# Queueing a block's gate-times-value product behind the next score's relu, loading the square-root table early, and turning the gains on TensorE

## The chip, the cores and the metric

The kernel runs on one core of one Trainium2 chip. The metric is the device time of one execution in microseconds (us). Most executions of one kernel lie here within a microsecond or two of each other; one first execution of the kernel before took 559.56 us. It is left out of every ratio, but the median of 443.69 us quoted below still counts it (the other three runs have 443.52). All runs recorded with a state are in the fast one. PE is the TensorE matmul engine, DVE is VectorE, ACT is ScalarE, SP issues most of the small transfers.

## The reference, cut to what matters

```python
# q, k, v: 8 batches, 12 heads, 448 positions, 64 wide
scores = q @ k.T / sqrt(64)
attn   = maximum(scores, 0) ** 2 / 448 @ v       # no softmax: relu, squared
x      = attn, heads side by side                # 3584 x 768
xn     = x / sqrt(mean(x * x) + 1e-6) * rms_g    # a norm over each row
g, val = xn @ w_gate, xn @ w_val                 # 768 -> 1536
out    = (silu(g) * val) @ w_out                 # 1536 -> 768
```

## The kernel before: the parts that matter

The kernel weaves two streams. While PE computes the gate and value blocks of batch b, pieces of batch b+1's attention are put between them. A block is one 128-wide slice of the 1536 hidden columns. It is 12 rounds of two matmuls, one for gate (psG) and one for value (psV), which run side by side on the two halves of the array's rows. In batches 1 to 7 it is issued in pieces of two rounds:

```python
def blocnpart(b, fb, r0, r1):
    if r0 == 0:
        gvs[b, fb] = [ps_m.tile([P, S], FP32, name=nm, tag="mm")[:] for nm in ("psG", "psV")]
    rounds(b, fb, gvs[b, fb], r0, r1)
    if r1 < 2 * KT:
        return
    psG, psV = gvs.pop((b, fb))
    s = spool.tile([P, S], BF16, name="sil", tag="sil")
    nc.scalar.activation(out=s[:], in_=psG, func=ACT.Silu)
    hT, o = hidden(b)
    nc.vector.tensor_tensor(out=hT[:, fb, o : o + S], in0=s[:], in1=psV, op=ALU.mult)
```

The pool `ps_m` has four buffers in PSUM, the memory that PE's results go to, so two blocks' worth: block n+2 takes the buffers of block n. A score has its own pool with two buffers; a relu empties it, on ACT, or on DVE for the second half of every odd head:

```python
    if on_dve:
        nc.vector.tensor_relu(out=r[:, cp], in_=src)
    else:
        nc.scalar.activation(out=r[:, cp], in_=src, func=ACT.Relu)
```

After a batch's attention, `leave` reads the last attention outputs on ACT, two pieces of an output projection follow on PE (their copies are on ACT), and then the norm: a square root on ACT, a reciprocal on DVE, six products of x, and DMAs that swap the halves of x into xD. The second six rounds of a block read xD.

## Time and profile before

| | before |
|---|---|
| median, first comparison | 443.69 us (4 runs, 443.1 to 559.56; 443.52 without the 559.56) |
| profiled execution | 443.02 us, span 441.2 us |
| first score on PE | 6.73 us |
| batches 1 to 7 on PE | 53.08, 49.11, 53.78, 49.12, 53.01, 49.12, 43.38 us |

A batch is measured on PE from the first instruction after one batch's output pieces to the first one after the next's. Odd batches carry four output tiles, even ones three, and batch 7 has no attention beside it. (The prediction's 53.85 us for batch 3 took the chain's entry at 242.40; PE's first score is at 242.33, so the length is 53.78.) The profile's lines are shown in the prediction.

### The profile page before, as it was taken

To read this page: it belongs to the slowest core of one execution; us is meant where nothing else is said; L and a number is where in the kernel's file an instruction comes from. 1 tells how busy PE (TensorE), PEld (TensorE's weight loads), DVE (VectorE), ACT (ScalarE), POOL (GpSimd) and SP (SyncE) were. 2 spreads that over 40 slices of the span, in tenths; PEclk is the share of its full clock that TensorE was granted. 3 is DMA by queue.
4 is the path that set the end of the run, shared out by engine and by line. 5 is a ranking of instruction groups with operands and counts; after the bars stand their busy time and mean duration, and the time that the engine had idled before them with its cause. 6 is when DMAs were issued, how large, how long until landed. Compare 5 with 4: busy or idle time off the path is not lost.

```text
span 441.2 us, 10928 instructions
## 1 busy us (share of the span) xinstructions
PE 431.9 (98%) x4718; PEld 248.6 (56%) x4718; DVE 288.8 (65%) x387; ACT 287.6 (65%) x445; POOL 53.7 (12%) x79
## 2 busy tenths in 40 slices
PE   7999999999999999999999999999999999999996
PEld 3345555655566555655566555655557555665664
DVE  4989975777863867766864768577775468742211
ACT  4899886676584775777765776767766677552220
POOL 8343300030001200021000300003000000000000
PEclk9999999999999999999999999999999999999999
DMA  9999999999117991189904997169903900041013
GB/s 135 196 207 198 197 211 186 199 177 182 33 37 157 208 153 33 37 182 169 149 15 96 188 207 95 36 108 224 164 18 78 206 20 1 1 116 57 1 37 109
DMA packets 87632, 53.21 MB, mean 121 GB/s; under 512 B 36768, under 2 KB 83232, under 8 KB 87584
## 3 DMA queue, kind: packets, MB, share of 16 engines
q0 software_dynamic: 44496, 27.50, 43.2%
q1 hardware_dynamic: 42464, 24.44, 28.1%
q8 instruction: 37, 0.61, 0.6%
q10 hardware_dynamic: 624, 0.57, 0.4%
q14 instruction: 11, 0.09, 0.1%
HBM read 47.19 MB, written 11.01 MB: 132 GB/s over the span
## 4 chain that ended last, share of the span: by engine, by line
PE 86%; ACT 7%; DVE 4%; issue 1%; DMA 1%; SPq 0%; ACTq 0%; DVEq 0%
PE psG L520 30%; PE psO L435 23%; PE psV L520 13%; PE psAV L273 9%; PE psS L228 6%; ACT r L217 2%; PE psW L663 2%; DVE r L240 1%; PE psS L187 1%; ACT r L197 1%; ACT sil L564 1%; DVE hT L566 1%; DMA xD<-xT 1%; DVE xT L500 1%; PE psT L143 1%
## 5 line engine op out<-in xcount | busy, mean ns | idle before, releaser
L520 PEld LDWEIGHTS <-wgv_sb 64*128 64x128 bf16 x2304 | 125.2, 94 | 95.6 <-issue 8.3
L520 PE MATMUL psV<-xD,wgv_sb 64*128 64x448 bf16 x558 | 128.4, 349 | 0.4 <-DMA xD<-xT 0.4
L520 PE MATMUL psG<-xD,wgv_sb 64*128 64x448 bf16 x558 | 128.5, 349 | 0.0
L520 PE MATMUL psG<-xT,wgv_sb 64*128 64x448 bf16 x558 | 128.4, 349 | 0.0
L520 PE MATMUL psV<-xT,wgv_sb 64*128 64x448 bf16 x558 | 128.0, 349 | 0.1
L242 ACT ACTIVATE r<-psS 112x896 bf16<-112x896 f32 x108 | 99.1, 918 | 20.5 <-PE psS L228 17.9
L435 PE MATMUL psO<-wo_sb,hT 128*64 128x512 bf16 (+2 forms) x1368 | 111.8, 323 | 0.0
L566 DVE TENSOR_TENSOR hT<-sil,psV 128x448 bf16<-128x448 bf16 x93 | 57.4, 618 | 62.6 <-ACT sil L564 62.6
L246 DVE TENSOR_TENSOR r<-r 112x1792 bf16<-112x1792 bf16 x72 | 78.0, 1088 | 29.2 <-ACT r L242 28.8
L435 PEld LDWEIGHTS <-hT 128*64 128x64 bf16 x1368 | 74.9, 110 | 35.6 <-issue 0.4
L564 ACT ACTIVATE sil<-psG 128x448 bf16<-128x448 f32 x93 | 50.5, 543 | 58.6 <-PE psV L520 35.5
L228 PE MATMUL psS<-qT,kT 64*128 64x448 bf16 (+1 forms) x288 | 56.1, 350 | 0.4
L587 ACT COPY ost<-psO 128x512 f32<-128x512 f32 (+1 forms) x54 | 25.1, 477 | 39.8 <-PE psO L435 39.8
L273 PE MATMUL psAV<-r,vb 112*64 112x448 bf16 x384 | 40.3, 355 | 0.0
L240 DVE TENSOR_SCALAR r<-psS 112x896 bf16<-112x896 f32 x36 | 39.0, 1084 | 1.9 <-PE psS L228 1.9
L175 POOL DMA_DIRECT2D qT<-qT x12 | 6.5, 541 | 263.5 <-PE psS L228 154.1
L273 PEld LDWEIGHTS <-vb 112*64 112x64 bf16 x384 | 20.1, 109 | 18.6 <-issue 6.5
L329 ACT ACTIVATE xT<-psAV,ga_sb 128x448 bf16<-128x448 f32 x47 | 27.8, 647 | 3.9 <-PE psAV L273 3.8
L228 PEld LDWEIGHTS <-kT 64*128 64x128 bf16 (+1 forms) x288 | 19.0, 97 | 16.0 <-issue 4.9
L500 DVE TENSOR_TENSOR xT<-xT,rstd 128x448 bf16<-128x448 bf16 x48 | 26.4, 619 | 2.3 <-ACT rstd L488 2.3
L471 DVE RECIPROCAL rhalf<-rhalf 128x224 f32<-128x224 f32 x8 | 12.4, 1553 | 21.3 <-ACT rhalf L465 21.3
L256 DVE TENSOR_TENSOR r<-r 112x1792 bf16<-112x1792 bf16 x23 | 24.3, 1083 | 0.7 <-ACT r L217 0.7
(68 smaller groups left out, 278.4 us busy)
## 6 DMA issues: line engine op xcount, KB each, us to landing
vb<-in_v_dram POOLq DMA_DIRECT2D x7, 672.0 KB, 18.4
xD<-xT SPq DMA_DIRECT2D x42, 112.0 KB, 2.3
qb<-in_q_dram POOLq DMA_DIRECT2D x6, 672.0 KB, 11.9
kb<-in_k_dram POOLq DMA_DIRECT2D x6, 672.0 KB, 14.5
qT<-qT POOLq DMA_DIRECT2D x24, 168.0 KB, 3.4
out_dram<-ost SPq DMA_DIRECT2D x7, 336.0 KB, 4.7
wgv_sb<-in_moe_w_gate_dram POOLq DMA_DIRECT2D x6, 384.0 KB, 16.9
wgv_sb<-in_moe_w_val_dram POOLq DMA_DIRECT2D x6, 384.0 KB, 16.9
```

Of the source, the lines that this page charges most:

```text
L228: nc.tensor.matmul(out=psS[: end - o, hf, :S], lhsT=flat[prt, o:end], rhs=qT[prt, 1 - hf : 3 - hf, h % HH], start=True, stop=True,)
L240: nc.vector.tensor_relu(out=r[:, cp], in_=src)
L242: nc.scalar.activation(out=r[:, cp], in_=src, func=ACT.Relu)
L246: nc.vector.tensor_tensor(out=r[:], in0=r[:], in1=r[:], op=ALU.mult)
L273: nc.tensor.matmul(out=part[hh * D : (hh + 1) * D, :], lhsT=ld["v", b][:, 2 * j + hh, c * D : (c + 1) * D], rhs=rsq[b, 2 * j + hh, c], sta ...
L329: nc.scalar.mul(out=xTs[b][:, j, :], in_=psAV[:, i, :], mul=ga_sb[:, j : j + 1])
L435: nc.tensor.matmul(out=ps[prt, :w], lhsT=lhsT[:, prt], rhs=rhs, start=start, stop=stop)
L500: nc.vector.tensor_tensor(out=x[:, kt, :], in0=raw_x[:, kt, :], in1=rstds[b][:], op=ALU.mult)
L520: nc.tensor.matmul(out=parts[part][:, :S], lhsT=wgv_sb[prt, h, fb * P : (fb + 1) * P], rhs=src[prt, kt, :], start=(r == 0), stop=(r == 2 * ...
L564: nc.scalar.activation(out=s[:], in_=psG, func=ACT.Silu)
L566: nc.vector.tensor_tensor(out=hT[:, fb, o : o + S], in0=s[:], in1=psV, op=ALU.mult)
L587: (nc.vector.tensor_copy if last else nc.scalar.copy)(out=osts[i, t][:, o : o + w], in_=ps[:, :w])
```

## The change

The intent: a score's relu should not wait on DVE behind a product that itself waits for silu. The diff holds two things more than that.

```diff
@@ leave: (b) the square-root table early
+        if b and js[-1] == HP - 1:
+            nc.scalar.activation(out=warm_act[:], in_=eps_col[:], func=ACT.Sqrt)
@@ blocnpart: (a) the product held for a piece
         rounds(b, fb, gvs[b, fb], r0, r1)
+        while held:
+            held.pop()()
         ...
-        nc.vector.tensor_tensor(out=hT[:, fb, o : o + S], in0=s[:], in1=psV, op=ALU.mult)
+        def product():
+            nc.vector.tensor_tensor(out=hT[:, fb, o : o + S], in0=s[:], in1=psV, op=ALU.mult)
+        if b > -1 and fb < FT - 1:
+            held.append(product)
+        else:
+            product()
@@ set-up: (c) the gains as rows, turned by PE
-        nc.sync.dma_start(out=g_sb[:], in_=moe_rms_g.rearrange("(kt p) -> p kt", p=P))
+        nc.sync.dma_start(out=g_rows[:], in_=moe_rms_g.rearrange("(kt p) -> kt p", p=P))
...
+    def columns_of_g():                      # called after the first transposes
+        psg = ps_m.tile([P, KT], FP32, name="psg", tag="mm")
+        nc.tensor.transpose(out=psg[:], in_=g_rows[:], identity=ident_g[:])
+        nc.vector.tensor_scalar_mul(out=ga_sb[:], in0=psg[:], scalar1=inv_attn)
```

More of the change, by code (lines that the diff above doesn't have):

```diff
@@ L565, in blocnpart @@
         hT, o = hidden(b)
-        nc.vector.tensor_tensor(out=hT[:, fb, o : o + S], in0=s[:], in1=psV, op=ALU.mult)
+        def product():
[4 more added lines that the diff above has]
+            product()
+    held = []
     osts = {}
@@ L633 @@
             eng.dma_start(out=first[nm][:], in_=head_rows(src, 0, 0, 2))
-        g_sb = wpool.tile([P, KT], FP32, name="g_sb", tag="rmsg")
-        nc.sync.dma_start(out=g_sb[:], in_=moe_rms_g.rearrange("(kt p) -> p kt", p=P))
+        g_rows = wpool.tile([KT, P], FP32, name="g_rows", tag="rmsg")
+        nc.sync.dma_start(out=g_rows[:], in_=moe_rms_g.rearrange("(kt p) -> kt p", p=P))
         load("k", 0, 2, 4)
@@ L650 @@
     ga_sb = wpool.tile([P, KT], FP32, name="ga_sb", tag="rmsga")
-    nc.vector.tensor_scalar_mul(out=ga_sb[:], in0=g_sb[:], scalar1=inv_attn)
+    ident_g = const.tile([KT, KT], FP32, name="ident_g", tag="ident_g")
+    nc.vector.tensor_copy(out=ident_g[:], in_=ident[:KT, :KT])
     load("k", 0, 4, 6)
@@ L697 @@
             fn()
+            if n == 0:
+                columns_of_g()
             if n % 3 == 2 and n < tail - 1:
```

## The prediction

> **What bounds the kernel now.** I read the page first: busy shares, then the chain that ended last. One engine carries the span, and the chain says the same: 86% of it is PE, 7% ACT, 4% DVE.
>
> ```profile
> PE 431.9 (98%) x4718; PEld 248.6 (56%) x4718; DVE 288.8 (65%) x387; ACT 287.6 (65%) x445; POOL 53.7 (12%) x79
> ...
> PE 86%; ACT 7%; DVE 4%; issue 1%; DMA 1%; SPq 0%; ACTq 0%; DVEq 0%
> ```
>
> 98% alone proves little, because ends of matmuls are modelled: a 448-column matmul shows 0.35 us while such pairs follow each other every 0.19 us. So a 0.23 us hole between starts can show as under 0.1 us of idle. I therefore measured PE from start to start. After 57 us, when the first batch's attention is done, only eight intervals exceed the usual 0.19 us by more than 0.15 us. Everything else there is work. Six of them are one pattern, once in each of batches 1 to 6, and the chain in order of time shows it at 107, 160, 210, 263, 312 and 365 us. Here is the one at 160 (start, length, what):
>
> ```profile
> 160.38 0.55 ACT sil L564
> 160.92 0.03 issue
> 160.94 0.62 DVE hT L566
> 161.57 1.01 DVE r L240
> 162.58 0.04 issue
> 162.62 0.36 PE psS L228 x2
> ```
>
> PE needs a score buffer; it comes free when the relu on DVE has read it; that relu stands in DVE's queue behind the product of a block (hT), and the product waits for ACT's silu. The timeline of PE shows the price: the last pair starts at 162.20 and the score at 162.62, 0.42 us instead of 0.19.
>
> ```profile
> 162.19 0.35 PE L520 MATMUL psG<-xD,wgv_sb 64*128 64x448 bf16 x1
> 162.20 0.35 PE L520 MATMUL psV<-xD,wgv_sb 64*128 64x448 bf16 x1
> 162.62 0.36 PE L228 MATMUL psS<-qT,kT 64*128 64x448 bf16 x2
> ```
>
> The other two intervals are at 191.78 and 192.72 us, at the head of batch 3, where PE waits for the swapped half of the normed x to land:
>
> ```profile
> 191.78 0.35 PE L520 MATMUL psG<-xD,wgv_sb 64*128 64x448 bf16 x1
> 192.33 0.35 PE L520 MATMUL psV<-xD,wgv_sb 64*128 64x448 bf16 x1 [0.20 <-DMA xD<-xT]
> ...
> 192.72 0.35 PE L520 MATMUL psG<-xD,wgv_sb 64*128 64x448 bf16 x1
> 193.29 0.35 PE L520 MATMUL psV<-xD,wgv_sb 64*128 64x448 bf16 x1 [0.22 <-DMA xD<-xT]
> ```
>
> They cost (0.55 - 0.19) + (0.57 - 0.19) = 0.74 us. As a check, from the chain's first score of each batch to the next, batch 3 takes 53.85 us (188.55 to 242.40) and its equals 1 and 5 take 53.08 and 53.01.
>
> **What the Trainium skill says.** "TensorE: Matmul & The Clock Gate", section "Wait — 56ns, not 53.3ns?", gives warm matmuls N / 2.4 GHz + about 2.5 ns start to start: 189 ns for 448 columns. The trace has 0.19, so PE's work between the holes is at its floor. The same page, section "Architectural detail", says that ACT and DVE run their queues strictly first in, first out; that is why queue order costs time at all, and the chain above agrees (the relu starts at 161.48, as the product ends, though its score started at 160.11). "ScalarE: Activation LUTs", section "What ACT_TABLE_LOAD costs", gives 1283 ns for a load and 2.66 us with a drain. The trace has 1283 ns as the mean of all loads, but no drain beside it: the load at 181.06 ends at 182.34 and the square root starts at 182.35. "DMA: Bandwidth & Descriptors", section "Specifications", wants 512 B or more per transfer for line rate; the gains vector is now read in 4-byte runs and took 4.0 us to land for 3 KB, which agrees.
>
> **The change part by part.** The diff holds three things, more than the words name.
>
> (a) *The product is queued one piece later.* No instruction is added or removed; what counts is which DVE instructions lie between the end of a block and the next piece. I wrote out the interleaving of pieces and attention steps from the program. In batches 1 to 6 only three of the eleven held products change place: block 2 and block 6 go behind the relu of head 3 and head 7, block 8 goes behind the squares of head 9. In batch 0 it is one relu and two squares; batch 7 has no attention beside it. Block 6 is the stall above. With the change the relu no longer waits for silu and product: DVE is free at 160.60 (squares end), the score started at 160.11, so the relu runs 160.6 to 161.7 by its 1.08 us. PE wants the buffer at 162.20 + 0.19 = 162.39, so 0.7 us of slack replace a wait of 0.23. The sum: 6 x 0.23 = **1.4 us**.
> The product itself then runs from 161.7 to 162.3 instead of 160.94 to 161.56. Its psV buffer is wanted by block 8, two blocks on, which starts at 163.19; 0.23 earlier is 162.96, so 0.6 us are left. Block 2 moves alike: relu at about 148.1 to 149.2, product to 149.8, block 4 begins at 150.60. Block 8: relu to 167.03, squares to 168.1, product to 168.7. Block 10 begins at 168.67, and 0.23 earlier with the rest of batch 2's saving. DVE's own start there follows PE's scores and also shifts, but the product lands **just about when its buffer is wanted**: a new wait of 0 to 0.3 us, six times at worst.
>
> (b) *A square root on one element after a batch's last attention output* brings the sqrt table in early. It replaces the load now at 181.06, so the count of loads stays; seven ACT instructions of 0.20 us are added. It is not free on ACT: load and small instruction, 1.28 + 0.20, begin when the last scaling ends (179.20), so the two copies of output pieces run at about 180.7 and 181.3 instead of 179.36 and 180.67, and the norm's square root comes at about 181.7 instead of 182.35. That is **0.65 us** earlier, not 1.28. The reciprocal (1.55), the six products of x (3.30) and the swaps follow it. PE's 0.74 us at 192 lie at the end of this very chain, so about 0.65 us of them go. In the five other batches the swap came in time, and the gain there is hidden.
>
> (c) *The gains come as 6 rows of 512 B and are turned by PE.* Added: one small transpose, one small DVE copy, the scaling moves behind the first qkT copies. PE has 0.64 us idle before its first score at 6.73 us (it waits for DVE's qkT), and DVE 0.65 us before its first relu at 7.33; both hold the added work (the old scaling took 0.17). Removed: 768 tiny DMA runs in the first 5 us. The trace lists ga_sb as the releaser of the first transposes at 5.50, but they follow the twelfth warm-up matmul by 0.28 us, just as a transpose follows a warm-up matmul later (0.29 at 10.50). The fixed warm-up is the gate, so I give this **0 us**, give or take 0.2.
>
> Sum: -1.4 - 0.65 + 0 = -2.05 us, plus an estimate of 0.2 for small new waits: **about -1.9 us**.
>
> **Rivals.** *The held product becomes the wait.* PSUM has four such buffers, two blocks' worth; the product now releases psV up to 1.1 us later. For: block 8's arithmetic above comes out at about zero slack, in each of six batches. Against: blocks 2 and 6 have 0.6 us or more, and the squares are often ready before the silu. If each of the six lost 0.3 us, 1.8 us come back and the time is 443.1. *The swap was an accident.* For: at batch 3 the swap DMAs' issue on SP took 1.52 us for the last one and left a 0.5 us hole before the third, while at batch 5 and 7 six took 0.5 to 0.6 each; at batch 4 one took 2.23 without harm to PE. If so, (b) saves nothing in a typical run: about 442.0. *The table load delays output copies until PE lacks a buffer.* Against: pieces of output take 2.6 and 1.3 us on PE, four buffers stand ready, and the copies slip by 0.7 to 1.3 us; no loss expected. *PE is simply the bound and nothing can move it 2%.* This is the frame of it all: all holes after 57 us that I found amount to about 2.2 us, 0.5% of the span. Only the first 57 us hold more, some 3 us of waits for relus and copies, and only (c) and three shifted products touch them.
>
> **Range and chances.** The two fast runs before are 443.1 and 443.5, the profiled one 443.0 (559.6 is an outlier that I leave out). From 443.3, less 1.9, I predict **441.4 us**. The low end, 440.2, is all of the 2.05 and a further microsecond from the start; the high end, 443.2, is the first rival, with hardly a gain. A change of 2% would be 8.9 us, four times all holes that the change can fill: faster 0.01, same 0.98, slower 0.01.
>
> **What will show it.** Right on (a): the chain no longer has silu, product, relu, score in a row once in a batch; on DVE the relu of head 7 precedes the product of block 6, and the PE interval before head 8's first score is 0.19. Batches 1 and 5 should shrink from 53.0 by about 0.23. Right on (b): the load before the norm's square root stands ahead of the two output copies, and the square root comes 0.6 to 0.7 earlier after the last attention output; no PE wait on the swap at batch 3. Right on (c): the first score still starts at about 6.7. I am wrong if PE waits on DVE's product at the start of blocks 4, 8 or 10, if a table load appears elsewhere, if the first score moves by over 0.3 us, or if the start shortens through lighter DMA traffic.

## The result, and the profile after

The changed kernel took **441.85 us** in the median (4 runs, 440.79 to 441.94), against 443.69 of the kernel before. The ratio is 0.9957, with a 95% interval of 0.9936 to 0.9979: about 0.4% faster, which is "same" by the 2% rule. A ratio here is the mean time of one kernel's fast runs over that of the other's of the same rounds, so it is not quite the ratio of the medians quoted.

The page of the changed kernel, its busy shares and its chain:

```profile
PE 431.6 (98%) x4719; PEld 253.1 (58%) x4719; DVE 287.7 (65%) x388; ACT 287.7 (65%) x452; POOL 53.7 (12%) x79
...
PE 92%; ACT 6%; issue 1%; DVE 0%; DVEq 0%
```

PE's busy time hardly moved; what changed is the chain. PE's share rose from 86% to 92%, DVE's fell from 4% to nothing, and ACT's went from 7% to 6%. What is left of ACT, 25.4 us, lies in the first 57 us; after them the chain is PE alone up to the last output copy. The DVE queue at the same place as in the prediction (start, length, instruction, names and shapes; idle time before it in brackets), first of the kernel before, then of the changed one:

```profile
160.94 0.62 DVE L566 TENSOR_TENSOR hT<-sil,psV 128x448 bf16<-128x448 bf16 x1 [0.34 <-ACT sil L564]
161.48 1.08 DVE L240 TENSOR_SCALAR r<-psS 112x896 bf16<-112x896 f32 x1
```

```profile
160.71 1.08 DVE L240 TENSOR_SCALAR r<-psS 112x896 bf16<-112x896 f32 x1
161.71 0.61 DVE L572 TENSOR_TENSOR hT<-sil,psV 128x448 bf16<-128x448 bf16 x1
```

The two have changed places, and the relu starts 0.77 us earlier on the clock. PE's timeline of the changed kernel there:

```profile
162.39 0.35 PE L522 MATMUL psG<-xD,wgv_sb 64*128 64x448 bf16 x1
162.39 0.35 PE L522 MATMUL psV<-xD,wgv_sb 64*128 64x448 bf16 x1
162.57 0.35 PE L228 MATMUL psS<-qT,kT 64*128 64x448 bf16 x2
```

The score follows the pair after 0.18 us; it was 0.42. All six such holes are gone. So are the two waits on the swap at batch 3. But there is one new thing, at the start of block 10, on PE and on DVE of the changed kernel:

```profile
168.44 0.35 PE L522 MATMUL psV<-xD,wgv_sb 64*128 64x448 bf16 x1
168.63 0.35 PE L522 MATMUL psG<-xT,wgv_sb 64*128 64x448 bf16 x1
168.76 0.35 PE L522 MATMUL psV<-xT,wgv_sb 64*128 64x448 bf16 x1
168.82 0.35 PE L522 MATMUL psG<-xT,wgv_sb 64*128 64x448 bf16 x1
168.95 0.35 PE L522 MATMUL psV<-xT,wgv_sb 64*128 64x448 bf16 x1
```

```profile
167.08 1.09 DVE L246 TENSOR_TENSOR r<-r 112x1792 bf16<-112x1792 bf16 x1
168.09 0.62 DVE L572 TENSOR_TENSOR hT<-sil,psV 128x448 bf16<-128x448 bf16 x1
```

In the kernel before, the product stood ahead of the squares, and the two matmuls of a pair at block 10 started 0.02 us apart:

```profile
168.67 0.35 PE L520 MATMUL psG<-xT,wgv_sb 64*128 64x448 bf16 x1
168.69 0.35 PE L520 MATMUL psV<-xT,wgv_sb 64*128 64x448 bf16 x1
```

```profile
166.95 0.61 DVE L566 TENSOR_TENSOR hT<-sil,psV 128x448 bf16<-128x448 bf16 x1
167.47 2.13 DVE L246 TENSOR_TENSOR r<-r 112x1792 bf16<-112x1792 bf16 x2
```

Now psV starts 0.13 us late: the product of block 8, behind the squares of head 9, ends at 168.71, and psV of block 10 takes its buffer at 168.76. No view calls this a wait, since PE goes on with the next gate matmul meanwhile. The lag stays to the end of the batch.

A lag of this kind is not new in itself. In batch 2 of all thirteen profiles, the kernel before among them, psV lags by 0.17 us from block 2 on, where it waits for the product of block 0 (which ends at 145.06 here):

```profile
144.94 0.35 PE L520 MATMUL psG<-xT,wgv_sb 64*128 64x448 bf16 x1
145.12 0.35 PE L520 MATMUL psV<-xT,wgv_sb 64*128 64x448 bf16 x1
```

The prediction's list did not have it, since no interval there reaches its 0.34 us, and no run here removes it.

From the first score to the last matmul the changed kernel takes 428.33 us, against 430.23: 1.90 us less. Its first score came later, at 7.17 instead of 6.73 us. Both need an explanation, and the three parts need to be told apart.

### The profile page after: what moved, and what is told of

It is laid out like the page before. It is cut to its first block, busy times and chain, and to the rows that moved or that the text cites. A ratio compares the mean times of both kernels' runs of the same rounds, so it can differ in the third digit from the quotient of the medians.

```text
span 440.0 us, 10930 instructions
## 1 busy us (share of the span) xinstructions
PE 431.6 (98%) x4719; PEld 253.1 (58%) x4719; DVE 287.7 (65%) x388; ACT 287.7 (65%) x452; POOL 53.7 (12%) x79
## 4 chain that ended last, share of the span: by engine, by line
PE 92%; ACT 6%; issue 1%; DVE 0%; DVEq 0%
PE psG L522 28%; PE psO L437 25%; PE psV L522 18%; PE psAV L273 9%; PE psS L228 6%; ACT r L217 2%; PE psW L682 2%; PE psS L187 1%; ACT r L197 1%; PE psT L143 1%; PE psS L207 1%; ACT qkT L151 1%; ACT gv L534 1%; PE psSS L463 1%; PE psE L522 0%
## 5 line engine op out<-in xcount | busy, mean ns | idle before, releaser
L522 PEld LDWEIGHTS <-wgv_sb 64*128 64x128 bf16 x2304 | 130.1, 94 | 93.1 <-issue 8.8
L228 PE MATMUL psS<-qT,kT 64*128 64x448 bf16 (+1 forms) x288 | 58.6, 349 | 0.0
```

The costliest lines, as they stand in the source:

```text
L228: nc.tensor.matmul(out=psS[: end - o, hf, :S], lhsT=flat[prt, o:end], rhs=qT[prt, 1 - hf : 3 - hf, h % HH], start=True, stop=True,)
L522: nc.tensor.matmul(out=parts[part][:, :S], lhsT=wgv_sb[prt, h, fb * P : (fb + 1) * P], rhs=src[prt, kt, :], start=(r == 0), stop=(r == 2 * ...
```

## The experiments

All eleven kernels gave correct results. "To the end" below is the time from first score to last matmul in the profile, start to start; batches are lengths on PE in us.

| kernel | median, ratio to before (95%) | to the end | batches 1 to 7 |
|---|---|---|---|
| before | 443.69 | 430.23 | 53.08 49.11 53.78 49.12 53.01 49.12 43.38 |
| before, again | 443.5, 0.9995 (0.9979 to 1.001) | 430.25 | 53.08 49.11 53.74 49.15 53.01 49.13 43.39 |
| product alone | 442.52, 0.997 (0.9953 to 0.9988) | 429.39 | 52.87 48.96 53.78 48.96 52.86 48.96 43.35 |
| table alone | 442.67, 0.9976 (0.9962 to 0.9991) | 429.29 | 53.01 49.11 53.01 49.13 53.01 49.13 43.25 |
| gains alone | 443.57, 0.9995 (0.9979 to 1.0011) | 430.55 | 53.08 49.11 54.09 49.12 53.01 49.12 43.38 |
| product and table | 441.48, 0.9958 (0.9946 to 0.9971) | 428.31 | 52.85 48.96 52.85 48.96 52.86 48.96 43.25 |
| changed | 441.85, 0.9957 (0.9936 to 0.9979) | 428.33 | 52.86 48.96 52.86 48.96 52.86 48.96 43.25 |
| changed, again | 441.53, 0.9961 (0.9948 to 0.9973) | 428.29 | 52.86 48.95 52.86 48.96 52.86 48.96 43.25 |
| only 2 and 6 held | 441.1, 0.9949 (0.9937 to 0.9962) | 427.60 | 52.73 48.84 52.74 48.84 52.73 48.83 43.25 |
| only 8 held | 443.36, 1.0002 (0.9989 to 1.0014) | 430.01 | 53.13 49.22 53.13 49.23 53.13 49.23 43.25 |
| held longer | 445.8, 1.0057 (1.0045 to 1.007) | 432.28 | 53.51 49.61 53.51 49.61 53.51 49.61 43.25 |
| 10 warm-ups | 441.68, 0.9972 (0.9958 to 0.9986) | 428.79 | 52.86 48.96 53.35 48.96 52.86 48.96 43.25 |
| 2 and 6, 10 warm-ups | 441.21, 0.9966 (0.9941 to 0.9992) | 427.58 | 52.74 48.84 52.74 48.84 52.74 48.84 43.25 |

The rows "before" and "changed" are of the first comparison. "Before, again" and each part alone ran beside before at 443.65 us, the others beside 443.09 us, each of these two sets on one chip. "To the end" leaves out what comes ahead of the first score and after the last matmul.

### Each part alone, and the kernel before again

The edits are the hunks (a), (b) and (c) of the diff, one at a time on the kernel before.

> The kernel before with the held product alone. Theory: this part carries most of the gain. In batches 1 to 6 the 0.42 us interval ahead of head 8's first score is back at 0.19 (6 x 0.23 = 1.4 us), less a new lag of psV behind psG of about 0.13 us from block 10 on, so batches 1, 2, 5 get 0.15 to 0.23 shorter and the kernel 1.0 to 1.3 us faster than before (ratio about 0.9975). The wait on the swap at batch 3, if it recurs, stays. Rival (the table load carries the gain): under 0.4 us.

> The kernel before with the early square-root table alone. Theory: the norm's square root comes 0.65 us earlier after the last attention output in every batch from 2 on, but PE gains only where it waited for the swap, at batch 3, if that wait recurs: 0 to 0.75 us (ratio 0.998 to 1.000); batches 1, 2, 4, 5, 6 keep their length of 53.0 and 49.1. Rival (it carries the gain): 1.2 us or more. Rival (it delays the output copies until PE lacks a buffer): batches longer by 0.2 or more, slower than before.

> The kernel before with the gains as six rows alone. Theory 1: it costs nothing; the 0.44 us by which everything ran later after the change came of the PE clock warming later in that one execution, so the first transpose starts at 5.5 or 5.75 independently of this part and the ratio is 1.000 within 0.001. Theory 2: it costs 0.2 to 0.45 us each time (first score at 7.0 to 7.2 in its profile, ratio about 1.001), through the transpose of the gains ahead of the first score. Rival (lighter DMA traffic shortens the start): first score ahead of 6.7.

> The kernel before, profiled a second time: ratio 1.000. It tells which of its holes recur. Expected: the six 0.42 us intervals ahead of head 8's scores recur exactly; the waits on the swap at batch 3 recur if they belong to the schedule (batch 3 at 53.8 us against 53.0 of batches 1 and 5) and vanish if a slow DMA issue on SP caused them; the first score starts at 6.73 or, where the clock warms later, up to 7.0.

**The product alone** made batches 1, 2, 4, 5 and 6 shorter by 0.15 to 0.21 us, and the run 0.3% faster. Batch 3 gained nothing. The waits of PE in this kernel (what waited for what, total us, times, longest) say why:

```profile
PE psV L520 <- DMA xD<-xT: 0.6, 1, 0.6
```

The wait on the swap took what the product had saved: PE arrived earlier, and the swap did not. So the two parts alone (0.84 and 0.94 us below) add up to 1.78 us, and together they save 1.92: only with the table does batch 3 gain from the product too.

**The table alone** took 0.77 us from batch 3, 0.13 from batch 7 and 0.07 from batch 1, and nothing from the others; the run was 0.24% faster. So its share is as large as the product's: 430.23 - 429.29 = 0.94 us against 430.23 - 429.39 = 0.84. My theory had allowed 0.75 at most, and no gain in batches 1 and 7. The wait on the swap is gone from this kernel's list.

**The gains alone** left the time as it was, within its interval of 0.16%. Its first score came at 7.20 us, as the theory of a cost had it; the next run shows that this proves nothing. Its batch 3 was slower (54.09), again by the wait on the swap, which here was 0.3 us longer.

**The kernel before again** showed the same six holes and again a long batch 3 (53.74). That alone would not clear the slow issue on SP that the prediction suspected, for it came again too: the last swap DMA of batch 3 took 1.54 us to issue, after 1.52 in the first profile. But of PE's two waits in the first profile only the second ends with the landing of that last DMA (193.25 us). The first ends with the fourth, which was issued in time and took 3.7 us to land (188.57 to 192.29); and the product alone, where no swap of batch 3 was slow to issue, has this wait too (its fourth took 4.1 us to land). So the wait at batch 3 belongs to the schedule: all four profiles without the early table have it. Its size varies. It also showed what the late first score is. First this second profile of the kernel before, then the changed one's, on PE:

```profile
4.50 1.33 PE L663 MATMUL psW<-warm_in 128*128 128x448 bf16 x3
5.75 0.58 PE L143 MATMUL psT<-ident,kb 112*64 112x112 bf16 x8
6.13 0.54 PE L143 MATMUL psT<-ident,qb 112*64 112x112 bf16 x8
7.18 0.36 PE L187 MATMUL psS<-qkT 64*128 64x448 bf16 x2 [0.50 <-DVE qkT L149]
```

```profile
5.75 0.58 PE L143 MATMUL psT<-ident,kb 112*64 112x112 bf16 x8
6.12 0.56 PE L143 MATMUL psT<-ident,qb 112*64 112x112 bf16 x8
6.61 0.22 PE L675 MATMUL psg<-ident_g,g_rows 6*128 6x6 f32 x1
7.17 0.36 PE L187 MATMUL psS<-qkT 64*128 64x448 bf16 x2 [0.34 <-DVE qkT L149]
```

The unchanged kernel has its first score at 7.18 too, without any transpose of the gains. In both, warm-up matmuls still follow each other every 0.37 us at the end, and the transposes take 0.58 us where the first profile of before had 0.39. The PE clock had not warmed yet: in the profile of the product alone the last warm-up matmuls follow each other every 0.19 us. "TensorE: Matmul & The Clock Gate", section "What's actually happening", says that the window which decides this runs free and does not start with the kernel. The profiles fit that: with twelve warm-up matmuls the first transposes begin anywhere from 5.10 to 5.75 us, in the kernel before at 5.51 and at 5.75, and the first score comes from 6.33 to 7.20. So the 0.44 us alone are no sign of the change: the kernel before does the same. It stays open whether the rows make a late start more likely. Of the six profiles with rows and twelve warm-ups, five began their transposes at 5.75 us; of the five without rows, one did. These are too few to tell from chance. The transpose itself fits in PE's idle time before the score: another kernel below that has it (only 8 held) began its transposes at 5.51 and its first score at 6.73, just as the first profile of before did.

### Which held product gains, and which loses

```diff
-        if b > -1 and fb < FT - 1:
+        if b and fb in (2, 6):        # other run: b and fb == 8
             held.append(product)
```

> The changed kernel, but only the products of blocks 2 and 6 of batches 1 to 7 are held; block 8's goes back ahead of the squares of head 9, as before the change. Theory: block 8's late product is what makes psV of block 10 lag psG by 0.13 us to the end of each batch, and that takes back 0.06 to 0.08 us in each of six batches. Expected: no lag at block 10, batches 1 to 6 at 52.80 and 48.88, some 0.3 to 0.5 us faster than the changed kernel in the trace from first score to last matmul. Rival (the remaining loss lies elsewhere): lengths stay 52.86 and 48.95.

> The changed kernel, but block 8's product alone is held. Theory: the gain of the held product comes from blocks 2 and 6, the loss from 8. Expected: the 0.42 us interval ahead of head 8's first score is back in six batches and the lag at block 10 stays: batches longer than the changed kernel's by 0.15 to 0.25, about 1.2 us slower than it, near the kernel before less the table's 1 us. Rival (block 8 matters and 6 does not): as fast as the changed kernel.

With 2 and 6 alone held, DVE has the product of block 8 ahead of the squares again, and PE's pairs at block 10 start together:

```profile
166.80 0.61 DVE L572 TENSOR_TENSOR hT<-sil,psV 128x448 bf16<-128x448 bf16 x1
167.33 2.13 DVE L246 TENSOR_TENSOR r<-r 112x1792 bf16<-112x1792 bf16 x2
```

```profile
168.53 0.35 PE L522 MATMUL psG<-xT,wgv_sb 64*128 64x448 bf16 x1
168.54 0.35 PE L522 MATMUL psV<-xT,wgv_sb 64*128 64x448 bf16 x1
```

Against the table alone, which has no product held, 2 and 6 are worth 0.27 to 0.30 us a batch (53.01 to 52.73), and 8 costs 0.10 to 0.12 (53.01 to 53.13). The sum is what the changed kernel shows (52.86, 0.15 less), so no other held product matters; nor do those of batch 0, which are not held here (79.63 us from the first score to batch 1 either way). So the lag of psV takes back **0.12 us in each of six batches, 0.73 us in all** (428.33 - 427.60). I had expected half of that, 0.06 to 0.08 a batch. With 8 alone held all six holes of 0.42 us are back, and the lag at block 10 is there (0.14); this kernel was 1.7 us slower to the end than the changed one, where I had expected 1.2.

No run holds 2 or 6 alone, but the traces of batch 2 part them, with 2 and 6 held against the table alone. From the start of block 7 to that of block 8, PE takes 2.65 us instead of 2.88: the gain of block 6. From block 3 to 4 it takes 2.65 instead of 2.83, but from block 4 to 5 4.54 instead of 4.39, since the lag of 0.17 us from block 2 now lasts through block 4. So nearly all of the gain is block 6's.

In the times, the version with 2 and 6 has the lowest median and ratio of all, but its interval overlaps the changed kernel's. Its profile shows that the part after the start of the last matmul took 5.20 us instead of 4.50, which in that execution takes back nearly all of the gain: the issue of the last stores on SP and ACT took 1.35 and 1.50 us where the changed kernel had 0.95 and 1.11. It came again: the other profile with 2 and 6 held, below, ends in 5.13 us, while the two of the changed kernel end in 4.50 and 4.41 and the two of before in 4.27 and 4.30. Why these issues vary is open, and two profiles each are few; but the end may go with the schedule, so a gain up to the last matmul need not be one of the whole.

### Holding longer

```diff
-        while held:
+        while held and r1 >= 6:       # three pieces into the next block
             held.pop()()
```

> The changed kernel with products held for three pieces of the next block instead of one. Theory (psV is released late): more products fall behind a relu or squares (blocks 2, 3, 7, 9 beside 8), PE waits for psV at the start of the blocks two further on, 0.1 to 0.5 us each; batches 1 to 6 longer by 0.3 to 1.2 us each than 52.86 and 48.96, 2 to 7 us slower than the changed kernel. Rival (release of psV isn't what block 10's lag comes from): lengths stay within 0.1.

Each of six batches became 0.65 us longer, and the run 0.57% slower than before. Now the wait is large enough to be listed:

```profile
PE psV L522 <- DVE hT L572: 1.4, 6, 0.2
```

PE waits for the buffer that the product releases, at two places in each batch (intervals of 0.59 and 0.36 us; the list shows only the larger ones, and shows them small because matmul ends are modelled). Late release of psV is a real cost, and one piece is already at its edge.

### Without the gains, and with a shorter warm-up

```diff
# product and table: hunk (c) left out of the change
# shorter warm-up, on the changed kernel:
-        warm(12)
+        warm(10)
```

> The changed kernel with the gains loaded as before (6 columns of 4-byte runs). Theory: the rows neither cost nor gain; expected within 0.1% of the changed kernel (ratio to before about 0.9957), the start decided by when the PE clock warms. Rival (the transpose of the gains costs 0.2 to 0.4 us): faster than the changed kernel by that.

> The changed kernel with 10 warm-up matmuls at the start instead of 12. Theory: the fixed warm-up, and not the gains or the casts, sets when the first transpose starts; with the gains as rows the casts of k and q end at about 4.9 and 5.25, so two matmuls fewer (0.37 us each while the clock is cold) bring the first transpose from 5.75 or 5.5 to about 5.0 and the first score forward by 0.3 to 0.6 us: 441.3 against 441.85. Rival (fewer matmuls let the clock warm later): transposes and scores run longer at the cold rate and nothing is gained, or 0.2 to 0.5 us lost.

Product and table without the gains equal the changed kernel: 428.31 against 428.33 us to the end, 441.48 against 441.53 us in runs on one chip. The rows show no cost or gain; the runs of each kernel scatter by 0.8 to 1 us, so one of 0.2 us, which would fall ahead of the first score, could hide there.

With ten warm-ups the first transposes began at 5.00 and the first score at 6.45, both at the cold clock's pace: 0.7 us ahead of a twelve-warm-up start that is as cold (7.17). The median did not show it (441.68 and 441.53, where I had expected 0.5 us less). In its profile part of the wait on the swap was back at batch 3 (53.35), although the table came early:

```profile
PE psV L522 <- DMA xD<-xT: 0.3, 1, 0.3
```

So the early table cleared this wait in eight of the nine profiles that have it, but with little to spare. In the ninth the last swap DMA took 4.1 us to land, where the one before it took 2.2; why is open.

### The changed kernel again, and both improvements together

> The changed kernel, profiled a second time beside the two below: batches 1 to 6 at 52.86 and 48.96 again with psV lagging psG by 0.13 us from block 10 on; no wait on the swap at batch 3 if the early table clears it for good (up to 0.5 us if it only nearly does); ratio to before 0.9957.

> Both improvements on the changed kernel at once: blocks 2 and 6 alone held, 10 warm-up matmuls. Theory: 0.73 us less from first score to last matmul (427.6), and a start earlier by up to 0.7 us where the clock warms late; 440.6 to 441.1, ratio to before about 0.994. Rival (the shorter warm-up gains nothing in the median, as e6_warm10's 441.68 suggests): 441.1, as with blocks 2 and 6 alone.

The second profile of the changed kernel repeats the first to 0.01 us in every batch, and has its first score at 7.18. Both improvements together have the shortest span of all profiles, 439.1 us, and add up in the trace as expected, up to the last matmul. Its median, 441.21 us, missed the 440.6 to 441.1 that I expected; it lies 0.3 us under the changed kernel's, but its six runs scatter from 440.73 to 444.41 and the ratio is no better. I can show the better schedule in the trace; a better time I cannot claim.

## Why the prediction was right, point by point

The time was 441.85 us for a predicted 441.4, in the range of 440.2 to 443.2. In the trace, first score to last matmul, the saving was 1.90 us for a predicted 1.9. The mechanism held, but two sizes were off, in opposite directions. That the sum came out at 1.90 is luck: block 8's loss was 0.53 us larger than my 0.2 for new waits, and the gains of (a) and (b) were together about 0.5 us larger than I had them.

- **PE is the bound, and only its holes can be won.** Right. All parts work through holes of PE measured from start to start, and PE's own work stayed at 0.19 us a pair.
- **(a) 6 x 0.23 = 1.4 us from the relu going first.** The pattern went where I said, and blocks 2, 6 and 8 are the ones that matter. Blocks 2 and 6 are worth a little more, 0.27 a batch, 1.6 us in six, nearly all of it block 6's, as I had it. Batches 1 and 5 were to shrink by about 0.23 us; they shrank by 0.22 and 0.15, because block 8 took some back.
- **"plus an estimate of 0.2 for small new waits".** Mis-sized. Block 8's arithmetic, "just about when its buffer is wanted", named the right place, and the lag is 0.13 us, which is one of the signs that I had named for being wrong (PE held up by the product at block 10), in small; but the lag costs 0.12 us in each batch, 0.73 us in all. I gave the sum 0.2 though my own "0 to 0.3 us, six times at worst" had 0.9 as its middle.
- **(b) 0.65 us.** Mis-sized the other way: 0.94 alone. Two terms failed. First, the square root came earlier by more than 0.65. ACT before, then after the change:

```profile
179.36 0.59 ACT L587 COPY ost<-psO 128x512 f32<-128x512 f32 x1 [0.16 <-PE psO L435]
180.67 0.37 ACT L587 COPY ost<-psO 128x256 f32<-128x256 f32 x1 [0.72 <-PE psO L435]
181.06 1.28 ACT L465 ACT_TABLE_LOAD   x1
182.35 0.45 ACT L465 ACTIVATE rhalf<-psSS,eps_col 128x224 f32<-128x224 f32 x1
```

```profile
179.27 1.28 ACT L333 ACT_TABLE_LOAD   x1
180.56 0.20 ACT L333 ACTIVATE warm_act<-eps_col 128x1 f32<-128x1 f32 x1
180.67 0.84 ACT L599 COPY ost<-psO 128x512 f32<-128x512 f32 x2
181.40 0.46 ACT L467 ACTIVATE rhalf<-psSS,eps_col 128x224 f32<-128x224 f32 x1
```

  It moved from 182.35 to 181.40, while the output pieces began at 176.56 and 176.62: 1.01 us earlier in the batch. I had added whole durations, 0.59 + 0.37, but back to back the two copies take 0.84, and the square root starts before they have ended. "ScalarE: Activation LUTs", section "What ACT_TABLE_LOAD costs", says that ACTIVATEs in a row overlap by about 93 ns; the small activation, the two copies and the square root overlap here by 0.10, 0.10 and 0.12 us, and I did not use it. That is enough for all of batch 3's 0.77 us. The swap gained more still: the fourth, for which PE waited first, was issued at 188.57 and landed at 192.29 before, and at 187.63 and 189.86 after, 0.94 us earlier out and 2.4 earlier in. Why the later transfer took 3.7 us and the earlier one 2.2 is open. Second, I called the gain in the other five batches hidden. Batch 7 had a wait on the swap too (an interval of 0.30 us at 396.62, under the 0.34 us that my list began at) and gave 0.13, batch 1 gave 0.07. A second interval of 0.31 us, at 398.26, is none of it: there psV of block 2 waits for DVE's product of block 0, and it stands in every kernel of this study.
- **(c) 0 us, give or take 0.2.** Right as far as whole times can tell: 443.57 alone against 443.65. The 4.0 us that I gave for the load of the gains say nothing of its 4-byte runs: loads of 112 to 224 KB beside it took 3.7 to 4.3 us to land. "Wrong if the first score moves by over 0.3 us" came true in the profile, 0.44, and would have misled: the kernel before does the same in its second profile.
- **The rivals.** The held product does become a wait, at about a tenth of a microsecond a batch. The swap's wait was no accident, though its size varies. No output copy delayed PE. Nothing moved 2%.

## What to carry to other kernels

In a program that is bound by one engine, list the intervals between that engine's starts and ask of each hole who stood ahead in whose queue; moving one instruction in a strict queue can fill it without adding work. Move only the instruction at the hole: the same rule applied to all blocks gave back almost half of that part's gain (0.73 us of 1.6) at a block where the held work was itself on time. And run the unchanged kernel under the profiler twice before explaining a difference at the start of a run.

## What the Trainium skill lacked or had wrong

- "TensorE: Matmul & The Clock Gate": it has the concurrency of row halves, but not that a lag between the two matmuls of a pair persists. Here a lag of 0.13 us at one buffer's release stayed to the batch's end and cost 0.12 us, without any wait listed; one of 0.17 us lasted from block 2 to block 3 or 4.
- "ScalarE: Activation LUTs": 1283 ns for a table load is right, but the drain of about 1.38 us beside it does not show. The load at 179.27 starts 0.01 us after the scaling before it ends and itself ends at 180.55, and the next instruction starts at 180.56.
- "DMA: Bandwidth & Descriptors": the page does not say how much the issue of one DMA on SP can vary. Here issues of the swaps took 0.5 to 0.6 us as a rule and up to 2.2 in the kernel before; in the changed kernel the stores had a median of 0.44 us, and one, at 143.21 us, took 2.4. Longer issues at the end went with an end up to 0.7 us later.
